# Moving casts, conversions and loads in the order of GpSimd's and the DMA queues' work, and rationing MoE pieces, in an attention-plus-MoE kernel

## Chip, cores, metric

One core of a Trainium2 chip. The metric is the device time of one execution in us, lower is better. Engines: PE (TensorE matmul), PEld (its weight loads), DVE (VectorE), ACT (ScalarE), POOL (GpSimd), SP (SyncE, here only the issuer of most DMAs). A run counts as slow when it lies over 1.5% above the fastest of the same kernel; ratios use fast runs alone.

## The reference

Attention with a decay, for 8 batches x 8 heads x 576 positions x 64, then a two-layer SiLU network on the 4608 tokens:

```
scores = q @ k.T / sqrt(D) + (cum_i - cum_j)      # causal, cum = cumsum(log f)
attn   = softmax(scores) ;  x = attn @ v           # -> [4608, 512]
h = x @ w_in ; g = h * sigmoid(h) ; out = g @ w_out   # 512 -> 2048 -> 512
```

The kernel folds the decay of j into v (v times a weight w), so that a division of num by den gives x.

## The kernel before

The schedule is written by hand: each engine runs its instructions in the order in which the program names them. The unit n is a pair of heads (four units per batch, 32 in all). Its work is: cast q and k to bf16 (`cast_qk`, GpSimd), transpose them (`transposes`, PE for batches 0 and 1, a DMA transpose from unit 8 on), four score chunks with their exponential (`scores`: PE, ACT, and masks on DVE). Each pair of units (m = n//2) then has `den` (PE, ACT copy), two reciprocals (`rec_part`, DVE), two `num` and two `divide` that write x transposed into xT.

MoE work fills PE's gaps: `fill(k)` emits k pieces of four 128x512 matmuls. A piece h (`m1_chunk`) multiplies xT by w_in, then ACT takes a tanh and DVE multiplies. A piece p (`m2_part`) multiplies by w_out. Tokens come in nine groups of 512, each with 16 h and then 16 p pieces. A group may start when its batch has been divided (`finished`).

```python
def fill(n):
    for _ in range(n):
        a, c = done["m1"], done["m2"]
        can1 = a < 16 * ready["g"] and a < 16 * (c // 16) + 32
        can2 = c < 16 * (a // 16) and ready["m2"]
        if not can1 and not can2:
            return False                       # nothing left: PE gets no filler
        if can1 and (not can2 or a - c <= 16 + (c % 2)):
            m1_chunk(...)                      # an h piece, preferred when it lags
        else:
            m2_part(...)                       # a p piece
# ... units 0 to 3; after unit 2:
            rec_part(0, 0); rec_part(0, 1)
            for c in range(NM + 1):
                convert_v(0, c, nc.gpsimd if c < 2 else nc.vector)
            load_w_in(0); load_w_in(1)
# ... den, num and divide of pairs 0 and 1, then
cast_qk(NP, POOLS); fill(3); transposes(NP); fill(1)
for n in range(NP, 2 * NP):                    # units 4 to 7
    scores(n, 0); scores(n, 1)
    if n + 1 < 2 * NP:
        cast_qk(n + 1, POOLS); transposes(n + 1)
    load_qk(n + NP)
    fill(1); scores(n, 2); scores(n, 3); fill(1)
    if n % 2 == 1:
        # unit 5 only: convert_v(1, c)
        den(m); rec_part(m, 0); rec_part(m, 1)
        for e in range(2):
            num(m, e); divide(m, e, nc.gpsimd)
        fill(2)
        # unit 5 only: load_w_out(i)
finished(2 * NP - 1)
# ... load_v(2); cast_qk and transposes of units 8 and 9 ...
for n in range(2 * NP, NU):                    # units 8 to 31
    scores(n, 0); scores(n, 1); fill(2)
    # ... loads, cast_qk(n + 2), transposes(n + 2), convert_v ...
    fill(2); scores(n, 2); scores(n, 3); fill(3)
    if n % 2 == 1:
        fill(1); den(m); rec_part(m, 0); num(m, 0); num(m, 1)
        fill(1); rec_part(m, 1); divide(m, 0, nc.gpsimd); divide(m, 1, nc.gpsimd)
        fill(2); finished(n)
while fill(1):
    pass
```

The softmax here doesn't subtract the row's maximum and nothing guards it: scores larger than these inputs give would overflow.

## Time and profile before

| | before |
|---|---|
| median of 4 runs | 416.35 us (414.69 to 418.48) |
| span of the profiled run | 415.0 us |
| PE busy | 353.4 us, 85% |
| unit 8's first scores on PE | 86.8 us |
| den to den, pair without / with a batch boundary | 20.37 / 22.7 to 25.0 us |
| last den to the end | 69.5 us |

Three rows of the page's table in 40 slices of 10.4 us (tenths of a slice busy; PEclk is the granted clock in tenths; the DMA row is the mean busy share of the 16 DMA engines):

```profile
PE   3648847469997999989998999899959996999996
...
PEclk9968996959999899989999999899988999799999
...
DMA  6999939993963974386466928490902011000112
```

PE has three weak stretches: the first nine slices, a dent each few slices, and one near the end, and the clock falls with each. The DMA row is full from slice 1 to 4, has a hole in slice 5 (52 to 62 us) and is full again until 93 us.

The view of waits, PE's own (us in total, times, longest):

```profile
PE hp L377 <- POOL xT L356: 15.6, 12, 3.9
PE sc L280 <- DMA qkT<-qkb: 8.9, 1, 8.9
PE tp L244 <- POOL qkb L112: 7.3, 1, 7.3
...
PE dn L327 <- DVE u L294: 4.4, 2, 3.4
```

The first is h pieces that wait for the division of their batch. The next two belong to the front. The timeline of all engines shows them (start, duration, engine, line, operation, in brackets how long the engine idled and what ended it):

```profile
57.56 2.80 POOL L356 TENSOR_TENSOR xT<-nm,rec 128x576 bf16<-128x576 f32 x2 [8.11 <-DVE rec L344]
...
60.31 3.10 POOL L174 DMA_DIRECT2D w_out_bf<-in_moe_w_out_dram  x4
63.38 0.65 POOL L112 CAST qkb<-qf 128x512 bf16<-128x512 f32 x1
...
64.09 1.04 PE L244 MATMUL tp<-ident_bf,qkb 128*128 128x128 bf16 x4 [7.29 <-POOL qkb L112]
```

GpSimd sat idle for 8.1 us because its next instruction was a division that needed DVE's reciprocal, while unit 7's cast, whose inputs it could have had earlier, stood behind that division and the issue of w_out. The same happened again before unit 8:

```profile
79.14 2.75 POOL L356 TENSOR_TENSOR xT<-nm,rec 128x576 bf16<-128x576 f32 x2 [14.33 <-DVE rec L344]
81.84 0.60 POOL L117 CAST qkb<-qf 128x512 bf16<-128x512 f32 x1
...
83.26 2.92 SPq L237 DMA_TRANSPOSE qkT<-qkb  x2
...
86.80 0.85 PE L280 MATMUL sc<-qkT 64*128 64x400 bf16 x6 [8.85 <-DMA qkT<-qkb]
```

A batch boundary on PE's timeline, and the granted clock around it (windows of 3.4 us: length, busy us of PE and the others with instruction counts, then PEclk, DMA share, GB/s):

```profile
130.83 0.60 PE L377 MATMUL hp<-xT,w_in_bf 128*128 128x512 bf16 x2
132.23 0.38 PE L377 MATMUL hp<-xT,w_in_bf 128*128 128x512 bf16 x1 [0.79 <-POOL xT L356]
133.63 4.65 PE L377 MATMUL hp<-xT,w_in_bf 128*128 128x512 bf16 x13 [1.03 <-POOL xT L356]
```

```profile
130.20:133.60 3.40, 1.61 (x11) 0.52 (x10) 1.84 (x3) 2.06 (x3) 2.83 (x3) 1.00 0.44 126
133.60:137.00 3.40, 3.37 (x9) 1.17 (x9) 1.23 (x3) 1.19 (x2) 3.40 (x6) 0.51 0.71 154
```

The first h piece waits twice, 0.79 and 1.03 us, for the two last quarters of xT. Then PE runs 3.4 us at half clock. So this boundary costs 1.8 us of waiting and 1.7 us of slow matmuls. Those at 176 and 264 us look the same; at 308 us, where the pieces have run out, the waits are 2.9 and 0.8 us. The end of the attention work, on PE:

```profile
348.03 0.60 PE L377 MATMUL hp<-xT,w_in_bf 128*128 128x512 bf16 x2
352.56 0.59 PE L377 MATMUL hp<-xT,w_in_bf 128*128 128x512 bf16 x1 [3.93 <-POOL xT L356]
353.92 0.59 PE L377 MATMUL hp<-xT,w_in_bf 128*128 128x512 bf16 x1 [0.77 <-POOL xT L356]
```

### The profile page before, as it was taken

Reading aid. Unit: us, or ns where it says so; the run is one execution under the profiler, and the core shown is the slowest. Engines: PE = TensorE matmul, PEld = TensorE weight load, DVE = VectorE, ACT = ScalarE, POOL = GpSimd, SP = SyncE. Lnnn points to the kernel's source line nnn. Section 1 sums busy time; section 2 is a strip of 40 time slices with the busy share of each in tenths; the row PEclk is TensorE's granted clock in tenths of the full one; section 3 lists DMA queues with packets and bytes.
Section 4 is the critical chain, followed back from the end, with each engine's and each line's share of the span. In section 5 each row is a group of like instructions: output and inputs, shape, how many; then the busy total and the mean of one; then the engine's idle time right before and its main releaser. Section 6 shows DMA issues by size and latency. Waiting matters only on the chain.

```text
span 415.0 us, 8554 instructions
## 1 busy us (share of the span) xinstructions
PE 353.4 (85%) x3427; PEld 169.2 (41%) x3469; DVE 236.5 (57%) x373; ACT 234.3 (56%) x360; POOL 138.0 (33%) x193
## 2 busy tenths in 40 slices
PE   3648847469997999989998999899959996999996
PEld 2426423224443444435453444344424443344442
DVE  4688974615765667466736871678246834473310
ACT  4744754427674667567756865486547753464421
POOL 3817542371233605090508240641346021100000
PEclk9968996959999899989999999899988999799999
DMA  6999939993963974386466928490902011000112
GB/s 186 227 207 214 190 65 171 194 148 84 219 142 94 185 148 100 87 191 134 102 160 116 207 73 191 105 210 11 235 27 57 2 52 52 0 2 25 51 52 76
DMA packets 141303, 49.74 MB, mean 120 GB/s; under 512 B 129424, under 2 KB 135568, under 8 KB 141264
## 3 DMA queue, kind: packets, MB, share of 16 engines
q1 hardware_dynamic: 134928, 44.99, 49.5%
q0 software_dynamic: 6336, 4.21, 6.5%
q8 instruction: 27, 0.44, 0.5%
q14 instruction: 12, 0.10, 0.1%
HBM read 36.85 MB, written 9.44 MB: 112 GB/s over the span
## 4 chain that ended last, share of the span: by engine, by line
PE 67%; DVE 8%; issue 6%; DMA 5%; ACT 4%; POOL 4%; SPq 3%; another core or an unknown queue 1%; POOLq 1%; ACTq 0%
PE hp L377 29%; PE po L404 27%; PE dn L327 6%; PE sc L280 5%; DVE rec L344 4%; POOL xT L356 3%; ACT rec L339 2%; DMA qf<-in_q_dram 2%; DMA vf<-in_v_dram 2%; ACT u L287 1%; DVE u L294 1%; SPq L88 1%; DVE qkT L251 1%; DMA qkT<-qkb 1%; SPq L130 1%
## 5 line engine op out<-in xcount | busy, mean ns | idle before, releaser
L377 PE MATMUL hp<-xT,w_in_bf 128*128 128x512 bf16 x549 | 149.0, 407 | 20.7 <-POOL xT L356 15.6
L386 DVE SCALAR_TENSOR_TENSOR gt<-th,hp 128x512 bf16<-128x512 bf16 x144 | 96.3, 684 | 67.7 <-ACT th L385 67.0
L404 PE MATMUL po<-w_out_bf,gt 128*128 128x512 bf16 x561 | 132.9, 381 | 1.2 <-issue 0.6
L385 ACT ACTIVATE th<-hp 128x512 bf16<-128x512 f32 x144 | 85.2, 604 | 83.7 <-PE hp L377 80.8
L287 ACT ACTIVATE u<-sc 128x800 bf16<-128x800 f32 x128 | 100.0, 839 | 33.0 <-PE sc L280 33.0
L356 POOL TENSOR_TENSOR xT<-nm,rec 128x576 bf16<-128x576 f32 x30 | 42.0, 1418 | 201.5 <-DVE u L294 100.1
L377 PEld LDWEIGHTS <-w_in_bf 128*128 128x128 bf16 x576 | 56.0, 103 | 92.3 <-issue 42.0
L294 DVE TENSOR_TENSOR u<-u,mask 128x256 bf16<-128x256 bf16 x128 | 56.6, 450 | 63.2 <-ACT u L287 62.3
L404 PEld LDWEIGHTS <-gt 128*128 128x128 bf16 x576 | 54.8, 98 | 66.0 <-issue 2.1
L344 DVE RECIPROCAL rec<-rec 128x288 f32<-128x288 f32 x32 | 61.0, 1933 | 20.2 <-ACT rec L339 20.2
L280 PE MATMUL sc<-qkT 64*128 64x176 bf16 (+5 forms) x512 | 35.2, 254 | 14.5 <-DMA qkT<-qkb 8.9
L413 ACT ACTIVATE osb<-po 128x512 f32<-128x512 f32 x36 | 21.6, 599 | 36.8 <-PE po L404 20.5
L221 POOL TENSOR_TENSOR vp<-vf,w_bf 128x512 bf16<-128x512 f32 (+1 forms) x37 | 38.1, 1044 | 2.7 <-DMA vf<-in_v_dram 1.8
L280 PEld LDWEIGHTS <-qkT 64*128 64x128 bf16 x512 | 18.4, 95 | 43.7 <-issue 26.2
L327 PE MATMUL dn<-u,vp 128*32 128x64 bf16 (+4 forms) x1152 | 29.7, 251 | 1.7
L327 PEld LDWEIGHTS <-vp 128*32 128x32 bf16 x1152 | 22.0, 101 | 7.9 <-issue 3.3
L351 ACT ACTIVATE nm<-dn 128x576 f32<-128x576 f32 x32 | 20.8, 650 | 7.1 <-PE dn L327 7.1
L244 PE MATMUL tp<-ident_bf,qkb 128*128 128x128 bf16 x64 | 10.9, 353 | 14.1 <-POOL qkb L112 7.3
L327 PE MATMUL dn<-u,w_bf 128*32 128x64 bf16 (+4 forms) x576 | 16.6, 248 | 5.2 <-DVE u L294 4.4
L339 ACT ACTIVATE rec<-dn 128x576 f32<-128x576 f32 x16 | 10.4, 650 | 13.7 <-PE dn L327 13.7
L327 PEld LDWEIGHTS <-w_bf 128*32 128x32 bf16 x576 | 11.1, 98 | 15.1 <-issue 10.8
L117 POOL CAST qkb<-qf 128x512 bf16<-128x512 f32 x24 | 14.8, 616 | 2.3 <-DMA qkT<-qkb 2.3
(42 smaller groups left out, 95.2 us busy)
## 6 DMA issues: line engine op xcount, KB each, us to landing
out_dram<-osb SPq DMA_DIRECT2D x36, 256.0 KB, 2.1
qf<-in_q_dram SPq DMA_DIRECT2D x64, 128.0 KB, 3.1
kf<-in_k_dram SPq DMA_DIRECT2D x64, 128.0 KB, 3.3
vf<-in_v_dram SPq DMA_DIRECT2D x32, 256.0 KB, 5.0
w_in_bf<-in_moe_w_in_dram POOLq DMA_DIRECT2D x8, 256.0 KB, 14.3
w_out_bf<-in_moe_w_out_dram POOLq DMA_DIRECT2D x4, 512.0 KB, 9.9
qktf<-in_q_dram SPq DMA_DIRECT2D x8, 128.0 KB, 3.4
qktf<-in_k_dram SPq DMA_DIRECT2D x8, 128.0 KB, 3.6
```

The lines of the kernel that those rows point to most:

```text
L221: eng.tensor_tensor(out=vp[r, c, :, :], in0=vst[b][c][r, :, :], in1=w_bf[r, c, b * H : (b + 1) * H, None].to_broadcast([n, H, D]), op=ALU. ...
L280: nc.tensor.matmul(sc[:, i, lo - c * CW : hi - c * CW], lhsT=t[r, k_off(kb) : k_off(kb) + P], rhs=t[r, q0 : q0 + hi - lo], start=True, sto ...
L287: nc.scalar.activation(out=u[:, :, c * CW : (c + 1) * CW], in_=sc[:, :, 0:CW], func=ACT.Exp, scale=scale)
L294: nc.vector.tensor_tensor(out=x, in0=x, in1=mask[:, None, :].to_broadcast([P, 2, P]), op=ALU.mult)
L327: nc.tensor.matmul(dn[HD * j : HD * (j + 1), q0:q1], lhsT=w, rhs=u_part(n, i, kb, q0, q1), start=(kb == 0), stop=(kb == NM or (kb == NM - ...
L344: nc.vector.reciprocal(out=recs[qd][:, r], in_=recs[qd][:, r])
L356: eng.tensor_tensor(out=xT[:, (2 * qd % NP) + e, b * S : (b + 1) * S], in0=nms.pop((qd, e))[:, :], in1=recs[qd][:, :], op=ALU.mult,)
L377: nc.tensor.matmul(hp[:, :], lhsT=w_in_bf[:, cc, fc * P : (fc + 1) * P], rhs=xT[:, cc, t0 : t0 + TG], start=(cc == 0), stop=(cc == NCC - 1),)
L385: nc.scalar.activation(out=th[:, :], in_=hp[:, :], func=ACT.Tanh, scale=0.5)
L386: nc.vector.scalar_tensor_tensor(out=gt[:, fc, :], in0=th[:, :], scalar=1.0, in1=hp[:, :], op0=ALU.add, op1=ALU.mult,)
L404: nc.tensor.matmul(po[:, :], lhsT=gt[:, fc, tb * P : (tb + 1) * P], rhs=w_out_bf[:, fc, :], start=(fc == 0), stop=(fc == NFC - 1),)
L413: nc.scalar.activation(out=osb[:, :], in_=po[:, :], func=ACT.Copy, scale=0.5)
```

## The change

Its intent: let GpSimd cast the next units before it divides, give GpSimd the whole first v conversion so that DVE is free for masks, load w_out directly behind the second batch's v, emit eight instead of nine MoE pieces per unit so that some are always left (the rationing), and release a new group only after the next unit's first scores and two pieces (the hold-back). Eight pieces are kept for the last division.

```diff
-    conv = ...tile_pool(name="conv", bufs=2)
+    conv = ...tile_pool(name="conv", bufs=3)
-    def transposes(n):
+    def transposes(n, evac=nc.vector.tensor_copy):     # both copies use evac
@@ units 0 to 3
         if n == 2:
             rec_part(0, 0)
-            rec_part(0, 1)
             for c in range(NM + 1):
-                convert_v(0, c, nc.gpsimd if c < 2 else nc.vector)
-            load_w_in(0)
-            load_w_in(1)
+                convert_v(0, c)
+                if c == 1:
+                    load_w_in(0)
+                    load_w_in(1)
+            cast_qk(NP, POOLS)
+    rec_part(0, 1)
     den(1)
@@
-    for m in range(2):
-        for e in range(2):
-            num(m, e)
-            divide(m, e, nc.gpsimd if m == 0 else nc.vector)
+    # num/divide of pair 0 on gpsimd, transposes(NP, nc.scalar.copy),
+    # num/divide of pair 1 on vector
@@
-    cast_qk(NP, POOLS)
-    fill(3)
-    transposes(NP)
-    fill(1)
+    cast_qk(NP + 1, POOLS)
@@ units 4 to 7
         if n + 1 < 2 * NP:
-            cast_qk(n + 1, POOLS)
             transposes(n + 1)
+        cast_qk(n + 2, POOLS)
+        if n == NP + 1:
+            for c in range(NM + 1):
+                convert_v(1, c)
+            for i in range(WQ):
+                load_w_out(i)
         load_qk(n + NP)
+        if n + 2 >= 2 * NP:
+            transposes(n + 2)
-        fill(1)
+        fill(2)
         scores(n, 2)
         scores(n, 3)
-        fill(1)
+        fill(2 if n % 2 == 0 else 1)
# (cut: in the odd units both num come first, then fill(1), then the divisions,
#  the second one on vector; convert_v(1), load_w_out, cast and transposes of
#  units 8 and 9 are gone from their old places, and so is finished(2 * NP - 1))
@@ units 8 to 31
         fill(2)
+        if p == 0:
+            finished(n - 1)
# (cut)
-        fill(2)
+        fill(1)
         scores(n, 2)
# (cut)
             fill(2)
-            finished(n)
+    fill(8)
+    finished(NU - 1)
     while fill(1):
```

## The prediction

> What bounds the kernel now. The span is 415.0 us, PE busy 85% of it (the page); the chain of waits is 67% PE. Where PE is fed, eight 128x512 matmuls follow each other in 1.73 us (chain). A piece of MoE work (four matmuls) thus costs 0.863 us, and the 288 pieces 249 us. By the timeline two score chunks take 0.56 us and a den or num group 0.84 us, so all PE work is about 340 us (estimate). The other 75 us are idle or half-clock time, in three places:
> 1. The front, 0 to 86.8 us. PE waits for DVE behind two 1.93 us reciprocals and three v conversions (den continues only at 28.98), then 7.3 us at 57-64 for casts behind divisions and the w_out issue on GpSimd, and 8.9 us before 86.8 for the DMA transpose of unit 8, whose cast comes behind the divisions.
> 2. Batch boundaries. A new group's first matmuls wait for the division: 0.79 + 1.03 us, and at four boundaries the next 11-13 matmuls take 4.6 us instead of 2.97. Pairs of units without a boundary take 20.37 us from den to den, with one 22.7-25.
> 3. The end. The last unit runs out of pieces, PE waits 3.9 + 0.8 us for the division, then runs about 4 us at half clock.
>
> The Trainium skill ("TensorE: Matmul & The Clock Gate", "The HAM clock gate") says that the array falls to half clock after an idle window of about 3.4 us and recovers after a busy one; the trace's 0.43 us matmuls after the stalls agree.
>
> What the change does. No arithmetic is added; work moves. GpSimd takes three conversions (1.04 us each against 0.65 on DVE), ACT the evacuation of unit 4's transposes, DVE some divisions (0.9 us). Casts and DMA transposes of units 8 and 9 come a unit or two earlier, w_out about 10 us earlier. Counting fill by hand: 16 m1 pieces before unit 8 in both; then 16 pieces per pair of units instead of 18, never starved; 8 pieces cover the last division; 80 remain after the last unit instead of 64.
>
> Sum, from trace durations:
> - Front: masks no longer wait for conversions (3 us), unit 4 no longer for four m1 pieces. Its scores start at about 35 us instead of 42. Units 4 to 7 took 27 us without the 7.3 us stall; plus four pieces (3.5 us) and DVE pressure (I count 33-35 us of DVE work): unit 8 starts at about 70 us instead of 86.8.
> - Units 8 to 31: 12 pairs x (20.37 - 2 x 0.863 = 18.65) = 224 us, plus about 5 for boundary waits left (the division ends 8.4 us after den starts, PE has 8.0 us of other work).
> - End: 80 x 0.863 = 69 us, plus 4 us for the last eviction, store and end.
> Span 372-375 us; the time lies 1.6 us above. I predict 376 us, 369 to 388. Chances: faster 0.95, same 0.04, slower 0.01.
>
> What would show it. Unit 8's scores at 67-75 us without a DMA wait; no 7 us wait for qkb; waits of PE for xT under 4 us instead of 15.6; den-to-den near 18.7 us; no half-clock matmuls after 80 us; DMA saturated without the gap at 52-62 us.
>
> What would make it wrong. DVE is over 90% busy in units 4 to 7 and may stretch them to 40 us. DMA must bring w_out, q, k and v by 70 us, about 70 us of saturated DMA by my estimate; late w_out would stall the first second-layer pieces. GpSimd holds conversions, casts and divisions in order: a late v stops all. One piece fewer between score chunks may expose ACT.

## The result

| | before | after |
|---|---|---|
| median of 4 runs each | 416.35 us | 372.25 us (371.67 to 374.30) |
| span of the profiled run | 415.0 us | 369.9 us |
| PE busy | 353.4 us, 85% | 340.9 us, 92% |
| mean granted clock | 0.937 | 0.991 |
| unit 8's first scores | 86.8 us | 71.1 us |
| den to den without / with a boundary | 20.37 / 22.7 to 25.0 us | 18.65 / 19.06 us |
| last den to the end | 69.5 us | 78.2 us |

The ratio is 0.8947 (95% interval 0.8893 to 0.9001). Ratios here are the mean time of one kernel's fast runs over the mean of the other's fast runs of the same rounds, so not quite the ratio of the medians. Both profiled runs are fast. All outputs are right.

The same rows of the page (a slice is 9.2 us now):

```profile
PE   2759877799999999999999999999999999999995
...
PEclk9987999999999999999999999999999999999999
...
DMA  6999999999968872896379737975220010001012
```

From slice 8 on PE is full in every slice but the last, and the clock never falls. The hole in the DMA row is gone. PE's waits:

```profile
PE hp L377 <- DVE qkT L251: 3.6, 3, 2.6
...
PE sc L280 <- DMA qkT<-qkb: 2.5, 1, 2.5
PE hp L377 <- POOL xT L356: 1.3, 5, 0.3
```

The wait for xT fell from 15.6 to 1.3 us, and the 7.3 us wait for a cast is gone. In the front, GpSimd now has unit 8's cast right behind the first division, and unit 8's scores start at 71.1 us; on the timeline of all engines:

```profile
50.23 3.10 POOL L174 DMA_DIRECT2D w_out_bf<-in_moe_w_out_dram  x4
...
53.39 1.40 POOL L356 TENSOR_TENSOR xT<-nm,rec 128x576 bf16<-128x576 f32 x1
53.48 1.92 DVE L356 TENSOR_TENSOR xT<-nm,rec 128x576 bf16<-128x576 f32 x1
...
54.74 1.13 POOL L117 CAST qkb<-qf 128x512 bf16<-128x512 f32 x1
...
57.29 1.02 PE L377 MATMUL hp<-xT,w_in_bf 128*128 128x512 bf16 x4 [2.65 <-DVE qkT L251]
...
71.09 0.52 PE L280 MATMUL sc<-qkT 64*128 64x400 bf16 x6 [2.51 <-DMA qkT<-qkb]
```

Two waits are left there: 2.65 us for DVE to evacuate unit 7's transposes, and 2.5 us for unit 8's DMA transpose. The first is in all six profiles with the changed front (2.65 us here, 2.44 or 2.45 in e1, e3, e4, e5 and r_after below). The second is not: e1 and e4 wait 0.4 and 0.6 us, e3, e5 and r_after not at all. These five start unit 8 at 69.6 to 74.2 us, so 71.1 is one draw of several.

A boundary, on PE's timeline, and the end of the attention work:

```profile
110.57 0.81 PE L377 MATMUL hp<-xT,w_in_bf 128*128 128x512 bf16 x3
111.65 0.38 PE L377 MATMUL hp<-xT,w_in_bf 128*128 128x512 bf16 x1 [0.27 <-POOL xT L356]
111.95 0.52 PE L280 MATMUL sc<-qkT 64*128 64x224 bf16 x10
```

```profile
291.75 0.87 PE L327 MATMUL dn<-u,w_bf 128*32 128x512 bf16 x36
...
295.98 7.93 PE L404 MATMUL po<-w_out_bf,gt 128*128 128x512 bf16 x36
303.75 7.93 PE L377 MATMUL hp<-xT,w_in_bf 128*128 128x512 bf16 x36
```

PE waits 0.27 us at a boundary instead of 1.8, stays at full clock, and at the end nine p pieces in a row (36 matmuls) cover the last division: the h pieces that need it follow without a wait.

Where the 45.1 us of span went can be added up from the starts of dens, if each piece that moved from one stretch to another is counted at 0.863 us:

| stretch | before | after | moved pieces | time won |
|---|---|---|---|---|
| start to unit 8's scores | 86.80 | 71.09 | 0 | 15.7 |
| to den of pair 4 | 18.01 | 13.45 | 2 (1.7 us) | 2.8 |
| to the last den | 240.72 | 207.21 | 17 (14.7 us) | 18.8 |
| to the end | 69.47 | 78.15 | -19 (-16.4 us) | 7.7 |

The sum is 45.0 us. The second row is the half-clock stretch that followed the 8.9 us wait.

### The profile page after: what moved, and what is told of

It reads as the page before. It is cut to its first block, busy times and chain, and to the rows that moved or that the text cites. A ratio compares the mean times of both kernels' runs of the same rounds, so it can differ in the third digit from the quotient of the medians.

```text
span 369.9 us, 8581 instructions
## 1 busy us (share of the span) xinstructions
PE 340.9 (92%) x3469; PEld 164.1 (44%) x3469; DVE 249.1 (67%) x368; ACT 233.7 (63%) x363; POOL 142.2 (38%) x195
## 4 chain that ended last, share of the span: by engine, by line
PE 69%; DMA 13%; DVE 6%; ACT 3%; POOL 3%; issue 3%; SPq 2%; POOLq 0%; ACTq 0%
PE po L404 30%; PE hp L377 29%; PE sc L280 5%; DVE rec L344 5%; DMA kf<-in_k_dram 5%; PE dn L327 4%; DMA qktf<-in_k_dram 4%; DMA qkT<-qkb 3%; ACT rec L339 2%; POOL xT L356 2%; DMA vf<-in_v_dram 1%; ACT u L287 1%; SPq L130 1%; SPq L83 1%; DVE qkT L251 1%
## 5 line engine op out<-in xcount | busy, mean ns | idle before, releaser
L377 PE MATMUL hp<-xT,w_in_bf 128*128 128x512 bf16 x576 | 139.7, 380 | 4.9 <-DVE qkT L251 3.6
L404 PE MATMUL po<-w_out_bf,gt 128*128 128x512 bf16 x576 | 139.7, 380 | 0.0
L294 DVE TENSOR_TENSOR u<-u,mask 128x256 bf16<-128x256 bf16 x128 | 70.8, 562 | 32.5 <-ACT u L287 30.6
L356 POOL TENSOR_TENSOR xT<-nm,rec 128x576 bf16<-128x576 f32 x28 | 39.3, 1425 | 134.6 <-DVE rec L344 125.1
L377 PEld LDWEIGHTS <-w_in_bf 128*128 128x128 bf16 x576 | 53.9, 98 | 68.2 <-issue 6.7
L404 PEld LDWEIGHTS <-gt 128*128 128x128 bf16 x576 | 53.4, 98 | 63.3 <-issue 2.0
L221 POOL TENSOR_TENSOR vp<-vf,w_bf 128x512 bf16<-128x512 f32 (+1 forms) x40 | 41.9, 1060 | 5.3 <-DMA vf<-in_v_dram 4.7
L280 PE MATMUL sc<-qkT 64*128 64x176 bf16 (+5 forms) x512 | 34.2, 250 | 7.7 <-DVE qkT L251 2.9
L327 PEld LDWEIGHTS <-vp 128*32 128x32 bf16 x1152 | 20.4, 99 | 10.2 <-issue 3.6
L117 POOL CAST qkb<-qf 128x512 bf16<-128x512 f32 x24 | 16.7, 694 | 0.0
```

The costliest lines, as they stand in the source:

```text
L221: eng.tensor_tensor(out=vp[r, c, :, :], in0=vst[b][c][r, :, :], in1=w_bf[r, c, b * H : (b + 1) * H, None].to_broadcast([n, H, D]), op=ALU. ...
L280: nc.tensor.matmul(sc[:, i, lo - c * CW : hi - c * CW], lhsT=t[r, k_off(kb) : k_off(kb) + P], rhs=t[r, q0 : q0 + hi - lo], start=True, sto ...
L294: nc.vector.tensor_tensor(out=x, in0=x, in1=mask[:, None, :].to_broadcast([P, 2, P]), op=ALU.mult)
L327: nc.tensor.matmul(dn[HD * j : HD * (j + 1), q0:q1], lhsT=w, rhs=u_part(n, i, kb, q0, q1), start=(kb == 0), stop=(kb == NM or (kb == NM - ...
L356: eng.tensor_tensor(out=xT[:, (2 * qd % NP) + e, b * S : (b + 1) * S], in0=nms.pop((qd, e))[:, :], in1=recs[qd][:, :], op=ALU.mult,)
L377: nc.tensor.matmul(hp[:, :], lhsT=w_in_bf[:, cc, fc * P : (fc + 1) * P], rhs=xT[:, cc, t0 : t0 + TG], start=(cc == 0), stop=(cc == NCC - 1),)
```

## The experiments

My theory: the gain has independent parts, the front (15.7 + 2.8 us), the boundaries (18.8 us) and the end (7.7 us); in the front it is the order on GpSimd and DVE, in the loop the hold-back that needs rationing to have something to do meanwhile. The rivals are stated with each run.

Runs e1 to e4, e5 to e8 and r_after to i3 are three jobs on three chips, each with the kernel before beside it. "Above the changed kernel" compares with the 372.25 us of the result, from a job of its own. The changed kernel, run again as r_after, gave 373.74 us (ratio 0.8990 instead of 0.8947), so a difference of 1 to 2 us across jobs says nothing.

### e1_front_only: the new front, the old loop

```diff
-        if p == 0:
-            finished(n - 1)
-        fill(1)          # between the score chunks
+        fill(2)
-    fill(8)
-    finished(NU - 1)
+            finished(n)  # after the odd unit's last fill, as before
```
(with `finished(2 * NP - 1)` ahead of the loop again)

> The new front (everything up to unit 8) with the old loop from unit 8 on: nine pieces per unit, a new group released at once, no pieces kept for the end. Theory: the two halves of the change are independent, the front is worth the 15.7 us that unit 8 starts earlier (86.8 to 71.1) plus up to 4.4 us of half-clock matmuls after 86.8: 396 to 401 us, with the old waits of PE for xT (about 15 us) back and half-clock stretches at the boundaries. Rival: the front only moves waiting into the DMA queue and the loop pays it back (w_out and q/k late): 405 to 416 us.

Measured: 396.39, 397.91 and 400.92 us (fast), 403.19 and 403.29 us (slow), ratio to before 0.9566. The profiled run was a slow one, so I take from it only PE's waits:

```profile
PE hp L377 <- POOL xT L356: 17.7, 13, 3.9
```

The front alone is worth 4.3%, or 18 us, and the boundary waits are back as they were. The theory's range holds the fast runs; the rival is out. The runs differ by 7 us; that the boundaries cause this spread was not tested.

### e2_loop_only: the old front, the new loop

The edit is the reverse: the diff's part for units 8 to 31, put into the kernel before.

> The old front with the new loop from unit 8 on (eight pieces per unit, group held back, eight pieces kept for the last division). Theory: 388 to 394 us, unit 8 still at about 87 us with its 8.9 us DMA wait, den to den 18.65 us and 19.1 at a boundary, PE waiting under 3 us for xT. Rival: the loop needs the early w_out and casts of the new front to run without waits: above 398 us with new waits in units 8 to 11.

Measured: 391.02 us (389.70 to 391.93), ratio 0.9416. PE's waits:

```profile
PE sc L280 <- DMA qkT<-qkb: 8.9, 1, 8.9
PE tp L244 <- POOL qkb L112: 7.3, 1, 7.3
...
PE hp L377 <- POOL xT L356: 1.8, 6, 0.5
```

The front's waits are those of before, the loop's are gone, pairs take 18.65 us. The two halves save 4.3% and 5.8%, together 10.2%; the whole change saves 10.5%. Within the intervals, front and loop are independent.

### e3_no_hold: rationed, but groups released at once

```diff
-        if p == 0:
-            finished(n - 1)
@@ end of the odd unit
+            if n < NU - 1:
+                finished(n)
```
(and `finished(2 * NP - 1)` ahead of the loop)

> The changed kernel, but each new group is released at the end of the odd unit as before, so its first piece h comes right after the scores of the next unit; still eight pieces per unit and eight kept for the end. Theory that the hold-back is what removes the boundary waits: five or six boundaries each wait about 1.3 to 1.8 us more, and some of them go to half clock for another 1.7 us: 380 to 390 us. Rival, that rationing alone does it because second-layer pieces are always left: under 375 us.

Measured: runs of 384.63, 387.33 (fast) and 392.79, 392.85 us (slow), ratio 0.9297, so 3.5% of the old time or some 14 us above the changed kernel. The fast runs lie inside the range, the slow ones above it. In the profiled run, a slow one, all five boundaries have the waits of before the change; den to den takes 20.78 us over the first and about 22.4 over the other four, against 19.07 in the changed kernel. One of them:

```profile
155.80 0.38 PE L377 MATMUL hp<-xT,w_in_bf 128*128 128x512 bf16 x1 [0.80 <-POOL xT L356]
157.20 0.38 PE L377 MATMUL hp<-xT,w_in_bf 128*128 128x512 bf16 x1 [1.03 <-POOL xT L356]
```

Rationing alone is not enough: `fill` prefers an h piece as soon as its group is released, although p pieces are there, and PE takes its instructions in order. The hold-back is what fills the wait.

### e4_nine: held back, but nine pieces per unit

```diff
-        fill(1)          # between the score chunks
+        fill(2)
```

> The changed kernel with nine pieces per unit again instead of eight (hold-back and the eight last pieces kept). By counting, pieces run out in units 24, 27, 28 and 31 and none is left for the last division. Theory that rationing matters only where pieces run out: no new wait before about unit 23, then waits of about 2, 4 and 4.5 us plus half clock: 380 to 388 us. Rival, that the hold-back alone is enough: under 375 us.

Measured: 389.56 us (389.04 to 391.73), ratio 0.9393, 17 us above the changed kernel and just above my range. On PE's timeline, in the last two batches:

```profile
280.94 0.58 PE L377 MATMUL hp<-xT,w_in_bf 128*128 128x512 bf16 x1 [2.52 <-POOL xT L356]
...
324.51 0.38 PE L377 MATMUL hp<-xT,w_in_bf 128*128 128x512 bf16 x1 [3.06 <-POOL xT L356]
325.87 17.14 PE L377 MATMUL hp<-xT,w_in_bf 128*128 128x512 bf16 x64 [0.98 <-POOL xT L356]
```

The waits came in the units where I had counted that pieces run out (1.8, 3.3 and 4.0 us, a little shorter than expected). What I had not expected are small losses at earlier boundaries: den to den 21.33 us at the first two instead of 20.37 without a boundary, where the changed kernel loses 0.41, because h pieces now follow each other in a row there and PE waits for DVE's product as well. So the hold-back without rationing runs dry, and rationing without the hold-back is not used. The two are one mechanism.

### e5_no_fill8: no pieces kept for the last division

```diff
-    fill(8)
```

> The changed kernel without the eight pieces kept for the last division. Theory: after the last den PE has about 5.7 us of work, the division ends about 8.4 us after den starts, so PE waits about 2.8 us (0.8 and 1.0 to 2 us), and up to 1.7 us more where that ends in a half-clock window: 2.5 to 4.5 us above the changed kernel, so 375 to 377 us. Rival, that the pieces are only moved and cost nothing: equal within 1 us.

Measured: 375.18 us (373.62 to 379.37, 6 runs, one of them slow; median of the fast ones 374.61), ratio 0.9032 (0.8990 to 0.9074). The median is in the range, but this interval overlaps those of both runs of the changed kernel (0.8893 to 0.9001, and 0.8949 to 0.9031), so the time alone does not separate theory and rival. The trace does, PE's timeline at the end:

```profile
298.57 0.38 PE L377 MATMUL hp<-xT,w_in_bf 128*128 128x512 bf16 x1 [1.34 <-POOL xT L356]
299.92 0.59 PE L377 MATMUL hp<-xT,w_in_bf 128*128 128x512 bf16 x1 [0.98 <-POOL xT L356]
```

The last den to the end takes 82.4 us here, 78.2 in the profiles of the changed kernel and of r_after, with the same 83 pieces: 4.2 us, of which 2.3 are these waits; behind them the granted clock is 0.59 for 4 us. Rationing leaves p pieces; without `fill(8)` the last group's h pieces go ahead of them and wait.

### e6_casts_behind: casts behind the divisions again, up to unit 9

```diff
-            cast_qk(NP, POOLS)          # after unit 2
@@ after divide(0, e)
+    cast_qk(NP, POOLS)
@@ units 4 to 7: moved from behind transposes(n + 1) to the end of the step
+        cast_qk(n + 2, POOLS)
+        if n + 2 >= 2 * NP:
+            transposes(n + 2)
```

> The changed kernel with the casts put behind the divisions again on GpSimd up to unit 9 (unit 4's cast after the first two divisions, units 6 to 9 at the end of their step), and the DMA transposes of units 8 and 9 with them. Theory that this order is what shortens the front: PE waits about 3.7 us for unit 4's cast, about 4 us for unit 7's, and 2 us or more for unit 9's DMA transpose: 378 to 384 us. Rival, that the front is bound by DMA anyhow and the order on GpSimd hardly matters: under 375 us.

Measured: 378.38 us (378.23 to 378.48), ratio 0.9109, 6 us above the changed kernel (5 above r_after). PE's waits:

```profile
PE tp L244 <- POOL qkb L112: 7.4, 2, 4.2
```

The two waits are 3.3 and 4.2 us, and unit 9's DMA transpose waits another 1.2 us. The theory holds: the order of casts and divisions on GpSimd is worth 5 to 6 of the front's 18 us.

### e7_v_on_dve: three v conversions back on DVE, ahead of the masks

```diff
             rec_part(0, 0)
+            rec_part(0, 1)
             for c in range(NM + 1):
-                convert_v(0, c)
-                if c == 1: load_w_in(0); load_w_in(1)
+                convert_v(0, c, nc.gpsimd if c < 2 else nc.vector)
+            load_w_in(0); load_w_in(1)
```

> The changed kernel with three conversions of the first v and both reciprocals of the first pair on DVE ahead of the masks, as before. Theory: the masks of unit 3 come about 3 us later and den with them (from 26.9 to about 29 us), and unit 4 starts 2 to 3 us later: 374 to 376 us. Rival, that GpSimd and the DMA are what the first division waits for, so DVE's work is hidden: within 1 us of the changed kernel.

Measured: 374.75 us (373.51 to 378.42, 6 runs), 2.5 us more than the changed kernel by the medians and 1.0 more than r_after. On PE's timeline den again continues at 29 us:

```profile
29.02 1.31 PE L327 MATMUL dn<-u,w_bf 128*32 128x512 bf16 x28 [3.66 <-DVE u L294]
```

The intervals of this ratio (0.8990 to 0.9074) and of the changed kernel's (0.8893 to 0.9001) just touch, and r_after's (0.8949 to 0.9031) overlaps, so the time does not decide against the rival; the wait itself is plain, 0.7 us in the changed kernel and 3.7 us here, and unit 4's scores start at 35.6 us instead of 34.4.

### e8_wout_first: w_out ahead of the second batch's v

```diff
     cast_qk(NP + 1, POOLS)
+    for i in range(WQ):
+        load_w_out(i)
@@ unit 5, behind convert_v(1, c)
-            for i in range(WQ):
-                load_w_out(i)
```

> The changed kernel with w_out issued right after unit 5's cast (at about 40 us instead of 50), ahead of the second batch's v. Theory that the DMA engines are saturated and the order decides: v of the second batch lands up to 5 us later, its conversions and den of unit 5 wait for it, unit 8 starts 2 to 5 us later: 374 to 378 us. Rival, that only the sum of the bytes counts: within 1 us, perhaps with the 2.5 us DMA wait of unit 8 gone.

Measured: 381.00 us (379.90 to 381.91, 5 runs), ratio 0.9171, 9 us above the changed kernel (7 above r_after), and unit 8 starts at 78.9 us. The direction was right, the size too small. PE's waits:

```profile
PE dn L327 <- POOL vp L221: 10.8, 5, 6.3
```

GpSimd issued w_out at 35.6 us, and the slowest load of v took 21.7 us from issue to landing instead of 11.5. GpSimd waited for it, and PE for the conversion. The Trainium skill ("DMA: Bandwidth & Descriptors", "Queues, rings and completion order") says that a DMA engine takes turns between the queues that have work. That fits: v stands in SP's queue, w_out in GpSimd's, and the trace shows v's landing about twice as slow; the turns themselves no run here shows. So w_out, which nobody needs before 71 us, belongs behind v, which PE needs at 48.

### r_after, i1, i2, i3: a second run of the change, and three attempts to beat it

The first is the changed kernel again. The next two take the two waits left in the front: DMA transposes of units 8 and 9 issued ahead of the loads of units 10 and 11, and ACT instead of DVE for the evacuation of unit 7's transposes (i1), or of units 6 and 7 (i2). i3 is i1 with w_out issued in two halves.

```diff
         if n + 1 < 2 * NP:
-            transposes(n + 1)
+            transposes(n + 1, nc.scalar.copy if n == NP + 2 else nc.vector.tensor_copy)   # i1
+            # i2: if n > NP
@@
+        if n + 2 >= 2 * NP:
+            transposes(n + 2)
         load_qk(n + NP)
-        if n + 2 >= 2 * NP:
-            transposes(n + 2)
```

> The changed kernel itself again, on the same chip as the three versions below, for a direct comparison and for its spread: 371 to 375 us, unit 8's scores between 69 and 75 us.

> An attempt to beat the changed kernel: the DMA transposes of units 8 and 9 are issued ahead of the q/k loads of units 10 and 11, and ACT instead of DVE evacuates unit 7's transposes. Theory: the 2.65 us wait of PE for the evacuation at 57 us goes, and the 2.5 us DMA wait of unit 8 where it occurs: 2 to 5 us below the changed kernel of the same job. Rival: DVE or the DMA backlog take the time back elsewhere in units 6 to 8: within 1 us.

> As the previous, but ACT evacuates the transposes of units 6 and 7. DVE is busy 31.8 of the 36.8 us of units 4 to 7 in the changed kernel, ACT 24.9, so moving 3.1 us of work balances them: theory 2 to 6 us below the changed kernel, up to 1 us better than the previous. Rival: ACT's exponentials of the scores come later and PE waits for them: no better than the previous.

> The first attempt, with w_out issued in two halves, the second one unit later behind unit 8's cast. Theory that the q/k loads and transposes then get through the DMA engines sooner: 0 to 2 us below the first attempt. Rival: the last quarter of w_out comes too late for the first second-layer pieces: 1 to 4 us above it.

| 6 runs each, one chip | median | range | ratio to before (95%) |
|---|---|---|---|
| r_after | 373.74 us | 371.50 to 376.05 | 0.8990 (0.8949 to 0.9031) |
| i1_order_act7 | 369.39 us | 368.08 to 371.89 | 0.8892 (0.8858 to 0.8927) |
| i2_order_act67 | 370.68 us | 368.39 to 373.92 | 0.8905 (0.8865 to 0.8945) |
| i3_split_wout | 371.85 us | 368.68 to 373.58 | 0.8949 (0.8915 to 0.8983) |

In i1, PE's wait for the evacuation is down to

```profile
PE hp L377 <- DVE qkT L251: 0.3, 1, 0.3
```

(3.1 us in r_after's profile), and unit 8 starts at 68.9 us against 71.6. i1 is 1.1% faster than r_after of the same job, and their intervals do not overlap: a small gain, and one that overlaps with the interval of the first result (0.8893 to 0.9001). i2, one of whose six runs is slow, is not better than i1: moving more to ACT brought nothing. i3 is no better either; its interval overlaps with i1's, so whether splitting w_out harms stays open. A DMA wait of unit 8 occurs in i1 (1.4 us), so the reordered issue does not rule it out, and the gain is best ascribed to the evacuation; this is argued, as the two edits were not run apart.

## Why the prediction was right

Predicted 376 us (369 to 388), measured 372.25.

- "unit 8 starts at about 70 us": 71.1, and 69.6 to 74.2 in five other profiles with that front. Unit 4's scores, predicted at about 35 us instead of 42, start at 34.4. Right.
- DVE pressure in units 4 to 7 (33 to 35 us of its work): DVE was busy 31.8 of the 36.8 us between, and one of the two waits left is on DVE. Right, and i1, which eases that wait, was a little faster.
- Unit 8's scores without a DMA wait: wrong in the profiled run (2.5 us), right in three others (0.4 and 0.6 us in the remaining two). The DMA row is full until about 100 us, so the front may be close to what the DMA engines can bring; no run with less traffic tested that.
- 12 pairs of 18.65 us: 18.65 exactly. The count of pieces was right, and PE sets the pace there (busy 266.1 of the 269 us from 80 to 349 us); that one piece fewer between score chunks would expose ACT did not happen.
- "about 5 for boundary waits left": this term was mis-sized. Five boundaries take 0.41 us each over a pair without one, 2.1 us in all.
- 80 pieces in 69 us, plus 4 us for the last store: right; no wait at the last division.
- Waits of PE for xT under 4 us, no half-clock matmuls after 80 us, no gap in the DMA at 52 to 62 us: 1.3 us, none, none.

The rest of the distance to 376 is that the sum gave 372 to 375 us of span and I named a time at its upper end. By stretches the sum said 70 + 229 + 73 us and the profile shows 71.1 + 225.8 + 73.1: the errors are small, and two of them have opposite signs. Some of the closeness is luck: the time that DVE pressure would add in units 4 to 7 was a guess and not worked out, and unit 8's start varies by 4.6 us between profiles.

The gains of front and loop add up (e1 and e2). Within the loop they do not: taking away the hold-back (e3) or the rationing (e4) each gives back 14 to 17 us, together more than the 26.5 us of loop and end, because each is of use only with the other. In the front, e6 (5 to 6 us) and e7 (at most 2 to 3 us, not clear of noise) account for less than half of the 18 us. The rest is argued from the timeline and was not undone by itself: the four h pieces that no longer stand before unit 4's scores, w_out's issue out of the casts' way, the third `conv` buffer, unit 4's evacuation on ACT and the divisions on DVE.

## What to carry to other kernels

In a hand-ordered schedule, look at each engine for an instruction that waits while a ready one stands behind it: here a division ahead of casts on GpSimd, and conversions ahead of masks on DVE (a plain wait, but its worth in time is not clear of noise). Filler work hides a wait only if it is still there and is ordered ahead of what waits, so ration it to the supply and hold the dependent work back; either half alone gave back 14 to 17 us. Count a stall on PE together with the half-clock time behind it, which here about doubled the price at most boundaries.

## What the Trainium skill lacked or had wrong

- "TensorE: Matmul & The Clock Gate", "HAM oscillation": it gives as a rule "no PE-idle gaps >~3.4µs". The 8.9 us stall before unit 8 agrees (granted clock 0.50 for the next 3.4 us). But two gaps of 0.79 and 1.03 us within one 3.4 us stretch (PE busy 1.61 of 3.40 us) were enough for a following stretch at half clock (0.51), in three of four such boundaries of the kernel before; at the fourth, at 222 us, 13 matmuls took 2.96 us. So the prediction's word that the trace agrees holds for the long stalls and not for these. The page's next section does tell of short, frequent idles that make the clock swing, but gives no length for them. The single gaps of 0.27 us in the changed kernel did not do it. The page's recovery after one busy window of about 3.4 us agrees (granted clock 0.50 from 133.8 to 137.0 us).
- "SBUF — State Buffer", "SBUF: two separate sides": it says that a DVE instruction with two SBUF inputs and a GpSimd instruction that reads SBUF exclude each other for the whole instruction. The trace agrees in kind: DVE's division at 53.5 us took 1.92 us beside GpSimd's of 1.40 us, against 0.84 us for the shortest of its four, and GpSimd's cast behind it took 1.13 us where most take about 0.6. The masks, which also have two inputs, rose from a mean of 450 to 562 ns in the changed kernel, which would fit if they now fall beside GpSimd's work more often (not tested). The page gives no durations for such pairs to plan with.
- No page read for this case says how much later a load lands when a second queue becomes busy; here the slowest v load went from 11.5 to 21.7 us.
